# Tying GpSimd casts to VectorE instructions in an attention and feed-forward kernel, with a new order of steps

## The chip, the cores and the metric

One core of one Trainium2 chip. The metric is the device time in microseconds (us) of one execution; three runs of the kernel before took 270.18, 269.0 and 268.93 us, median 269.0 us. One further execution was recorded by the profiler; all durations below are from that one.

The core has a matrix engine (PE), a vector engine (VectorE, DVE in the profile), a scalar engine (ScalarE, ACT), a general engine (GpSimd, POOL) and a queue engine (SyncE, SP) which here only issues DMAs. Each engine works through its own list of instructions strictly in order; semaphores join the lists.

## The reference

Attention over 4 batches x 8 heads, 768 positions, head size 64, with a block mask (blocks of 32: neighbours, first and last rows and columns, three sampled blocks per row), then a feed-forward layer on the 3072 tokens of width 512:

```python
scores = np.where(mask, scale * q @ k.T, -1e9)          # per batch and head
attn = exp(scores - max) / (sum + 1e-9)
x = (attn @ v)                                          # 3072 x 512, heads side by side
h = x @ w_in                                            # 512 -> 2048
g = h / (1 + exp(-beta * h))
out = g @ w_out                                         # 2048 -> 512
```

## The kernel before, in words

**Pairs and units.** The 32 heads are worked in 16 pairs (two heads side by side in the 128 partitions). The query rows of a batch are cut in two tiles of 256 and 512 rows; one pair's one tile is a *unit*, numbered 0 to 31 in the order of work. Feed-forward groups are numbered 100 to 106 (100 has 256 tokens, 101 to 105 have 512, 106 has 256).

**What one pair needs first** (`add_prep`, `add_half`, `add_load`, `add_cast`): k, q and v of the pair are loaded by DMA from the SP queue into float32 staging buffers `st_k` (4 of them), `st_q` (3), `st_v` (2). A *cast* (`add_cast`, its instruction on line 509 when GpSimd does it) makes float16 of each: `s16_k` and `s16_q` (the trace calls them s_k, s_q) or `va` (v). For pairs 0 to 3 PE transposes s_k and s_q and a copy puts them in `kX`, `qX` ("turn", "turn cp"); for the later pairs a transposing DMA on the SP queue does it (`turn` in `add_half`, line 524). A staging buffer can be loaded anew once its cast is done, so a cast also lets a later load go. The first later loads are held back by one-element GpSimd copies ("shut", line 489), which wait for the weights `w_out` to land.

**A unit** (`tile_steps`, `add_step`, `add_tail`): PE makes scores `sc` from kX and qX ("sc", 64 rows deep); ACT takes the exponential to `et` ("ex"); DVE multiplies `et` by the 0/1 mask ("mk": two float16 inputs, both in SBUF); PE multiplies by `va` ("av"); DVE takes the reciprocal of the sums and scales ("norm": its large input is in PSUM) to `xst`; a transpose brings that to `x`. The first four units add the mask on PE instead, with `shut_qk`.

**A feed-forward group** (`add_moe`, `add_mixed`): "hp" on PE (x by w_in, to PSUM), "th" on ACT (tanh), "gm" on DVE (`g`: one input t_sb in SBUF, the other in PSUM), then products with w_out. Groups 101 to 106 use a seven-product scheme for 2 x 2 blocks: DVE makes sums of halves ("sg": two SBUF inputs, one output of `s` or `g`) and, once, of the weights ("tw": two SBUF inputs, `w_mix` and `w_out_sb`); products ("pr") go to PSUM and are copied or added to `osb` ("cv", on ACT or DVE); the store goes by the SP queue (line 787).

**What sets the order.** No scheduler runs at build time. All steps are nodes with numbers; the table `STEPS` (from line 42) lists them in one sequence, and each engine gets its own steps in that sequence. A word of the table is the node's number, a letter for the engine (P PE, A ACT, D DVE, G GpSimd, S SP) and the buffer slots that it takes: `1041G3` is node 1041 on GpSimd in slot 3. `2V4`/`4W4` are filler matmuls on zeros (512 or 64 columns wide) near the start. Which engine does a step where two can (casts: D or G; PSUM copies: D or A) is thus also in the table. Helpers of class `Tap` record each PE, ACT and DVE instruction as it is emitted (line 185, which is why most instructions of the profile have that line); the GpSimd instructions are emitted directly.

**Nodes that the prediction names.** 54: cast of q of pair 3; 51 and 55: PE transposes of k and q of pair 3; 56: the copy of the latter to qX; 106, 107: last scores of unit 2 and their exponential; 113, 114: first scores of unit 3 and their exponential. 6: copy of a part of the mask on GpSimd (line 416); 209: a DVE copy to x; 236: the first "shut" copy; 237: the load of k of pair 4, 238 its cast on DVE. 620 and 623: casts of k and q of pair 8; 640, 641, 642: load, cast and transposing DMA of k of pair 9; 624: transposing DMA of q of pair 8; 669: the first scores that need it. 1041, 930, 927, 900: four casts which GpSimd does one after the other from 153.64 us on.

Of the kernel before, what the change touches and what calls it, by code (L numbers as in the profile page):

```python
# [42 lines left out]
11S0 15S0 19S 23S 27S1 0D 29S1 12D3 16G1 2V4 4W4 1P2 1W4 13P7 3D 2D 14A2 33S2 37S0 39S3 20G 43S1  # L43
1W4 17P6 18A 4W4 4P1 5D 1V4 4W4 80P3 81A2 7D 24D 2V4 1W4 21P0 22D 25P1 1V4 4W4 82P1 30D3 34D0 8D
26A 83Aa 28G1 47S1 1V4 2W4 84P0 85A0 31P7 32D0 38G2 9P5 35P4 44G0 36D 49S0 53S2 86P6 91P1 92A8
57S0 59S1 93P0 94Ad 87Db 10D 40D0 41P5 88D2 45P4 95P3 42D3 63S0 96A7 46D 104P1 102P0 89P5 103Ae
97P7 54G1 55P6 48D0 90A2 105A3 50D2 51P4 75G 76G 67S2 106P0 107A2 98De 99D0 100P7 52D1 56D 113P2
60D2 115P1 101D 117P3 61P0 62D 114A9 71S1 116A7 118Ab 108P1 184P1 185A2 68D1 64G0 65P0 187P2
109Dd 110D0 66D 193P3 69P1 190P1 77G 78G 79G 188Ad 58D3 119P4 186D 70D 196P0 189D 120Da 121D4
191A3 194A0 195D 199P3 122P2 111P5 112D 197A8 200Ab 210P2 123D 216P1 213P0 198D 201D 192D 211A7  # L50
212D 214Ae 215D 124P7 125A1 126D1 127P6 128A2 130P4 131A4 202P5 129D 133P1 217A6 132D 203D8
204D1 205P0 206Df 207D 136P6 134A4 135D 219P1 137A1 72D2 218D 138D 139P7 142P0 145P5 151P4 220Aa
140A5 143A3 141D 148P3 146A0 144D 152A5 149A6 147D 73P2 74D 153D 150D 221D 222P3 223A8 225P0
154P5 155A2 156D 224D 157P4 158A6 159D 226Ab 227D 169P2 160P7 170A1 161A5 162D 163P5 208P6 166P3
209D2 167A2 168D 247P0 164A3 165D 248A5 6G 236G2 237S 228P4 229D7 253P3 231P3 250P0 230D1 171D
256P2 254Ad 255D 232De 233D 251A8 249D 252D 172P2 257A4 258D 262P0 259P3 260Aa 240G0 178P3 173P
263A9 281P3 284P2 282A0 287P0 179P 174P 180P 261D 363D 364D 244G0 241S 296P3 238D1 367D 365D
283D 285Ae 290P2 288A2 264D 286D 293P0 239S3 297Ac 294A7 291A3 245S 273S3 175P 181P 268P1 265P7
234P6 176A1 235A 182A0 242D2 298D 289D 243S 276S0 279S1 295D 292D 299P2 368D 269Dc 266D3 267D2
270D 300D9 301D3 246G0 274G3 275S0 307S0 183S 310S2 302P0 404P2 407P3 303D7 304D 305P2 271P3  # L60
405A4 410P0 413P2 366D 306D 272D 318P3 315P2 408A5 406D 409D 369D 321P6 411A3 412D 277D2 414Ab
419P2 416P0 316A2 278S 280D1 319A0 317D0 320D 324P7 308G3 309S2 322A5 417A8 323D 418D 415D 327P2
333P0 330P6 313S0 429S2 432S0 336P1 420Ac 437P2 325A4 326D 328A1 329D 440P1 421D 334A5 331A2
332D 339P7 337A1 311G1 312S 422P6 335D 338D 371D0 423D1 424D2 438A1 441A2 442D 340A3 341D 342P4
446P1 443P0 345P5 348P6 343A0 444Ad 351P7 449P0 314G3 430G1 344D 354P4 346A1 347D 439D 425P5
447Ae 452P1 349A5 352A6 450A6 462P0 448D 433G2 350D 357P6 353D 360P7 355A2 453Ab 465P1 463A0
468P0 358A5 451D 426Dg 427D 445D 356D 454D 464D 455P5 458P4 361A2 359D 466A7 469Ac 362D 474P1
471P3 472A8 456D7 457D1 459Db 460D 374D 377P5 477P0 475A9 431S1 435S0 434S 487P3 478Ad 370D 473D
470D 467D 476D 479D 380P4 381P 490P1 488Aa 489D 372D 375D 493P0 491A3 378P 480P6 494Ae 379A0
481D2 382D 482D4 496P1 497A1 499P0 483P7 388P 502P1 500Ab 596P0 484Dh 485D 593P3 503A5 385P  # L70
594Ad 597A8 386P 599P1 600A0 606P3 619S3 622S2 428S0 607A9 623G1 620D0 389P 387A 436G2 492D 383D
504D 498D 495D 501D 595D 598D 376D 373D 505P1 506D6 609P1 612P3 508P0 610A7 391P 613A4 509D0
507D2 510D 627P1 625S1 640S1 461S 643S0 486S 644G2 641G1 646S0 177S 390D1 628A6 633P0 634Ab
630P3 631Ae 392P 601D 602P3 626G0 384D 614D 393D 603D8 604D0 394P 648P3 661S0 664S1 665D0 649A5
651P1 652A1 629D 653D 654P0 655A0 395P 621S3 511S 515P6 516A0 512P7 513A1 642S2 624S 669P0 396D
672P1 673Aa 397P 670A3 518P4 519A5 632D 611D 514D1 605S1 667S1 645S 682S3 685S2 662G0 663S1 666S
683G2 686G1 684S0 524P3 525A2 521P1 522A6 527P0 656D 608D 517D 520D 528A1 526D 523D 529D 530P4
531A6 690P3 691A8 671D 532D 635D 675P1 398P 615P0 676Ac 399D 692D 402S 616D0 617D2 618S 687S
401S 533P4 534A1 535D 693P3 694Ad 695D 696P1 697A7 636P1 668G3 688S1 536P0 537A1 637Da 638D0
538D 677D 539P7 540A3 706P1 703P2 704A2 542P1 543A2 707A4 545P0 546A4 548P5 551P4 554P2 552A5  # L80
549A0 557P3 541D 544D 674D 650D 560D0 647G1 555A3 547D 716P0 709P3 553D 657P4 689G2 558A4 710A9
550D 678P5 717A0 556D 559D 722P1 658Dg 659D2 719P3 566P4 567P 810P0 723A1 816P1 720A6 813P3
811Aa 711D 563D 679Dd 680D3 569P5 698D 699P0 570P 561D 564D 705D 721D 700D9 701D1 817A5 819P1
814A8 825P0 822P3 820A3 400S 403S 568D0 574P 708D 712P3 573D 571D 577P 823Ae 835P3 660S 681S
# [133 lines left out]
def kernel(  # L218
# [11 lines left out]
    nc = tc.nc  # L230
# [770 lines left out]
```

## Time and profile before

| what | us |
|---|---|
| median of three runs | 269.0 |
| the profiled execution | 269.45 |
| its span, first to last instruction | 267.6 |
| PE busy | 255.8 |
| DVE busy | 234.1 |
| ACT busy | 208.0 |
| POOL busy (58 instructions) | 41.4 |

The span and the execution's time differ by 1.85 us, which lie around the span. The granted PE clock is 1.00 throughout. "Busy" of PE counts modelled ends of pipelined matmuls, so it says where PE stands idle, and not how well it is filled. In a row of the time-ordered view stand start, duration, engine, line, operation, output<-input with sizes and types, the count, and in square brackets the idle time ahead of it with what ended it.

### The profile page before, as it was taken

How to read it: one execution, taken by the hardware profiler on the slowest of the kernel's cores; microseconds unless marked ns; L12 is line 12 of the kernel's file. 1: busy time of each engine (PE TensorE's matmuls, PEld its weight loads, DVE VectorE, ACT ScalarE, POOL GpSimd, SP SyncE). 2: the span in 40 equal slices, each digit the busy share in tenths (PEclk: the TensorE clock that was granted, in tenths of full speed). 3: DMA queues.
4: the chain of work that ended last, by engine and by line, in shares of the span. 5: the costliest groups of instructions: out<-in, count | busy, mean ns of one | idle time of the engine just before them, and what ended most of it. 6: DMA issues, size and time to landing. Idle time of an engine off the chain costs nothing.

```text
span 267.6 us, 6834 instructions
## 1 busy us (share of the span) xinstructions
PE 255.8 (96%) x2796; PEld 167.6 (63%) x2796; DVE 234.1 (87%) x483; ACT 208.0 (78%) x277; POOL 41.4 (15%) x58
## 2 busy tenths in 40 slices
PE   8987999999998999999999979999999999999994
PEld 4664873634465765556775536746676875578883
DVE  5548999999999989999999999789989996999762
ACT  2789999799997989898889867987587895643330
POOL 4334001203233020500006060200010000000000
PEclk9999999999999999999999999999999999999999
DMA  6999996999892899954499816800261100202042
GB/s 186 294 204 207 211 207 155 212 244 235 168 276 68 237 123 192 173 186 118 101 168 230 217 20 153 143 11 0 58 200 31 23 4 0 71 20 100 0 159 78
DMA packets 72979, 36.70 MB, mean 137 GB/s; under 512 B 29796, under 2 KB 68980, under 8 KB 72948
## 3 DMA queue, kind: packets, MB, share of 16 engines
q1 hardware_dynamic: 69744, 32.06, 52.4%
q0 software_dynamic: 3136, 4.19, 9.2%
q8 instruction: 22, 0.36, 0.6%
q14 instruction: 9, 0.07, 0.1%
q10 hardware_dynamic: 68, 0.01, 0.0%
HBM read 27.27 MB, written 6.29 MB: 125 GB/s over the span
## 4 chain that ended last, share of the span: by engine, by line
PE 71%; DVE 17%; ACT 6%; DMA 2%; issue 1%; POOL 0%; DVEq 0%; ACTq 0%; POOLq 0%
PE sc L185 71%; DVE et L185 6%; DVE g L185 4%; ACT et L185 3%; ACT t_sb L185 3%; DMA st_q<-in_q_dram 2%; DVE s L185 2%; DVE xst L185 2%; DVE w_mix L185 1%; DVE w_out_sb L185 1%; DVE recip L185 1%; DVE x L185 0%; DVE s_q L185 0%; DVE osb L185 0%; ACT osb L185 0%
## 5 line engine op out<-in xcount | busy, mean ns | idle before, releaser
L185 ACT ACTIVATE et<-sc 128x1024 f16<-128x1024 f32 x144 | 139.1, 1039 | 17.5 <-PE sc L185 16.3
L185 PE MATMUL sc<-x,w_in_sb 128*128 128x512 f16 (+1 forms) x448 | 90.1, 349 | 1.9 <-DVE g L185 1.7
L185 DVE TENSOR_TENSOR et<-et,mask 128x960 f16<-128x960 f16 (+1 forms) x132 | 85.7, 679 | 4.7 <-ACT et L185 4.7
L185 ACT ACTIVATE t_sb<-sc,beta_c_sb 128x512 f16<-128x512 f32 (+1 forms) x112 | 65.5, 644 | 25.6 <-PE sc L185 22.1
L185 DVE SCALAR_TENSOR_TENSOR g<-t_sb,sc 128x512 f16<-128x512 f16 (+1 forms) x112 | 64.0, 604 | 8.3 <-ACT t_sb L185 8.0
L185 PEld LDWEIGHTS <-w_in_sb 128*128 128x128 f16 x448 | 41.8, 98 | 40.4 <-issue 7.5
L185 PEld LDWEIGHTS <-g 128*128 128x128 f16 x505 | 47.1, 99 | 19.8 <-issue 9.2
L185 PE MATMUL sc<-w_out_sb,g 128*128 128x256 f16 (+1 forms) x384 | 50.9, 282 | 0.2 <-DVE xst L185 0.2
L185 PE MATMUL sc<-qX,kX 64*128 64x256 f16 (+1 forms) x384 | 45.6, 326 | 1.6 <-ACT et L185 0.8
L185 PEld LDWEIGHTS <-et 128*128 128x128 f16 x1152 | 40.9, 98 | 6.8 <-issue 3.2
L185 PE MATMUL sc<-va,et 128*128 128x65 f16 x1152 | 43.3, 193 | 1.3 <-ACT et L185 0.7
L185 PEld LDWEIGHTS <-kX 64*128 64x128 f16 x384 | 16.3, 94 | 18.5 <-issue 14.1
L509 POOL CAST va<-st_v 128x768 f16<-128x768 f32 x13 | 12.5, 963 | 88.9 <-PE sc L185 58.0
L185 PE MATMUL sc<-w_mix,s 128*128 128x256 f16 x176 | 22.1, 273 | 0.7 <-ACT osb L185 0.5
L185 DVE TENSOR_TENSOR xst<-sc,recip 128x256 f16<-128x256 f32 x48 | 19.7, 421 | 1.2
L185 PEld LDWEIGHTS <-s 128*128 128x128 f16 x176 | 16.2, 98 | 5.4 <-issue 3.7
L509 POOL CAST s_q<-st_q 128x768 f16<-128x768 f32 (+2 forms) x13 | 11.7, 901 | 21.1 <-DMA st_q<-in_q_dram 17.2
L185 ACT COPY osb<-sc 128x512 f32<-128x512 f32 (+2 forms) x14 | 7.5, 539 | 8.5 <-PE sc L185 8.5
L509 POOL CAST s_k<-st_k 128x768 f16<-128x768 f32 (+1 forms) x11 | 9.9, 904 | 24.1 <-DMA st_k<-in_k_dram 24.1
L185 DVE TENSOR_TENSOR osb<-osb,sc 128x512 f32<-128x512 f32 (+1 forms) x18 | 11.4, 635 | 2.2 <-ACT osb L185 1.4
L185 PE MATMUL sc<-w_mix,g 128*128 128x256 f16 x88 | 11.1, 273 | 0.0
L185 DVE RECIPROCAL recip<-sc 128x4 f32<-128x4 f32 x48 | 8.1, 173 | 2.9 <-PE sc L185 2.7
(66 smaller groups left out, 106.2 us busy)
## 6 DMA issues: line engine op xcount, KB each, us to landing
st_v<-in_v_dram SPq DMA_DIRECT2D x16, 384.0 KB, 4.3
out_dram<-osb SPq DMA_DIRECT2D x23, 256.0 KB, 2.5
st_k<-in_k_dram SPq DMA_DIRECT2D x15, 384.0 KB, 4.8
st_q<-in_q_dram SPq DMA_DIRECT2D x12, 384.0 KB, 4.8
w_in_sb<-in_moe_w_in_dram POOLq DMA_DIRECT2D x2, 1024.0 KB, 10.9
w_out_sb<-in_moe_w_out_dram POOLq DMA_DIRECT2D x2, 1024.0 KB, 19.2
st_q<-in_q_dram SPq DMA_DIRECT2D x12, 128.0 KB, 5.7
st_k<-in_k_dram SPq DMA_DIRECT2D x3, 128.0 KB, 2.5
```

Source lines behind the costliest of these rows:

```text
L185: r = f(*a, **kw)
L509: e(out=at(dst)[:, :, :, 0:D] if nm == "v" else by_chunk(dst, lo, hi), in_=src)
```

## The change

Three things. GpSimd instructions of the casts and of the mask copies are recorded too (`pool`). While the steps are emitted, the last DVE instruction so far is kept in `after`; a GpSimd cast or mask copy then gets a dependency on it, so that it can't start before that DVE instruction is done. And the whole table STEPS is another one: nearly the same sequence, in which steps of all engines stand a few places earlier or later, other buffer slots are taken, and some steps change engine. The core of the diff:

```diff
+    pool = Tap(nc.gpsimd, log)
...
-            e = dve if eng == "DVE" else nc.gpsimd
+            e = dve if eng == "DVE" else pool
...
-            e = dve.tensor_copy if eng == "DVE" else nc.gpsimd.tensor_copy
+            e = dve.tensor_copy if eng == "DVE" else pool.tensor_copy
...
+    after, told = None, mybir.DependencyInfo(mybir.DependencyClass.Sync,
+                                             mybir.DependencyReason.DATA)
     with tc.manual_schedule():
         emit_first()
         for n in seq:
...
+            if n.on == "DVE":
+                after = log[-1]
+            elif n.on == "POOL" and n.port and log and after is not None:
+                tc.add_manual_dep(log[0], after.name, told, reason="beside PSUM readers")
```

Of the table, the lines around the steps that the prediction names (before, then after):

```diff
-97P7 54G1 55P6 48D0 90A2 105A3 50D2 51P4 75G 76G 67S2 106P0 107A2 98De 99D0 100P7 52D1 56D 113P2
+40D2 57S1 91P3 93P2 92A0 94A2 86P1 87Da 59S0 41P0 45P7 95P1 42D1 46A 63S1 96Ad 102P2 106P3 103Ac
+88D1 104P0 50D3 89P3 97P2 67S2 76G 60G0 51P5 55P4 90D0 98D5 99D4 105Ab 52D3 77G 78G 79G 56A
+107A1 113P1 114Aa 71S0 115P0 117P2 116A6 118A0 61P6 100P7 108P2 58D3 64D1 65P3 62D 184P0 101D
...
-209D2 167A2 168D 247P0 164A3 165D 248A5 6G 236G2 237S 228P4 229D7 253P3 231P3 250P0 230D1 171D
+166P7 221D 223A1 224D 155A0 156D 158A2 159D 226Ab 227D 167A4 169P6 208P5 160P4 161A5 162D 209D2
+247P0 163P3 228P2 6G 236G3 237S 248A9 168D 253P2 250P0 231P7 170A2 164A1 229D8 230D2 254A7 171D
...
-270D 300D9 301D3 246G0 274G3 275S0 307S0 183S 310S2 302P0 404P2 407P3 303D7 304D 305P2 271P3
+279S0 307S2 274G1 275S1 295D 246G1 308G3 277G2 175P 176A0 180P 181P 182A1 268P2 365D 269Dc 368D
...
-775A0 770D 873D 889P2 758D 886P4 761D 864G0 865S 589S 773D 1015P0 1040S1 1041G3 930G0 592S 834S0
-859S 1043S0 591S 916P3 1016A2 927G0 928S0 1042S2 764D 917Ac 776D 783P5 1021P0 1022Ae 887Dd 888D1
+755D 756P3 746D 857Dg 899S1 862S3 926S1 927G3 591S 865S 929S0 932S0 834S1 592S 589S 928S0 895S1
+858D 759P0 767D 768P1 914Aa 915D 757A3 758D 897G2 771P2 762P3 774P7 930G0 885D 898S 911A2 769A4
+760A2 772A0 761D 770D 773D 763A3 764D 775A4 886P0 887Dh 776D 889P6 900G3 888D3 890Dd 891D 777D0
```

Steps that change engine: fifteen casts and copies of the first 40 us change between ACT and DVE or between DVE and GpSimd. Later, seven casts of whole k, q or v (128 x 768) go from GpSimd to DVE (436, 623, 644, 689, 861, 1041, 1047) and three from DVE to GpSimd (277, 280, 665); eight copies of a PSUM result (128 x 512) to osb go from DVE to ACT and three from ACT to DVE; one smaller one and two of three copies to x go from ACT to DVE, the third from DVE to ACT. The load order on the SP queue is the same for the first 18 loads. The fillers go from 7 wide and 21 narrow ones to 5 wide and 26 narrow ones. The number of matmuls that do work, of exponentials, multiplications and DMAs is the same.

More of the change, by code (lines that the diff above doesn't have):

```diff
@@ L120 @@
[L120 to L125 removed]
+11S3 12D3 0D 15S2 16D1 19S 23S 24G 20G 27S0 29S2 33S0 37S1 5W5 13P4 4V5 1W5 1P7 3D 14D0 2W5 9P0
@@ new lines @@
+1116P1 1119P0 1117D3 1118D4 1120D0 1121D 1234P3 1235Ad 1237P2 1238A5 1003P 1122P0 994D 1005P
+1244P3 1207D 1123D 1247P0 1250P2 1245Aa 1006P 1248A0 1239D 1210D 1213D 1214P6 1004D 1215Da
+1216D3 1220D 1007D 1236D 1223D 1124P1 1125A6 1127P7 1145P0 1128A0 1146A3 1251A3 1157P3 1008P
+1139P6 1166P4 1126D1 1226D 1233D 1129D 1158A2 1147D 1227P0 1136P5 1130P1 1228D2 1249D 1229D1
+1159D 1167A1 1217S2 1142P7 1140A6 1141D 1131A3 1137A4 1132D 1240P0 1241Db 1009P 1010A 1138D
+1143A4 1133P3 1169P2 1170A5 1134A2 1154P1 1252D 1242D4 1246D 1243S 1230S 1253P0 1168D 1160P4
```

144 lines of the change are left out of this document (66 added, 78 removed).

## The prediction

> **What bounds the kernel now.** I read the page's busy shares, its chain that ended last, that chain in order of time, and wherever it leaves PE, the time-ordered rows of DVE and POOL.
>
> ```profile
> PE 71%; DVE 17%; ACT 6%; DMA 2%; issue 1%; POOL 0%; DVEq 0%; ACTq 0%; POOLq 0%
> ...
> 85.19 64.41 PE sc L185 x712
> ...
> 164.87 31.34 PE sc L185 x282
> ...
> 202.54 56.35 PE sc L185 x604
> ```
>
> From 85 us on, PE sets the end in long runs (start, length), and what lies between them is what can be won. The largest hole of PE there is 1.73 us ahead of 159.61; DVE, POOL and PE around it (start, duration, engine):
>
> ```profile
> 152.68 1.27 DVE L185 SCALAR_TENSOR_TENSOR g<-t_sb,sc 128x512 f16<-128x512 f16 x2
> 153.98 1.03 DVE L185 TENSOR_TENSOR s<-g 128x1024 f16<-128x1024 f16 x1
> 155.05 1.20 DVE L185 TENSOR_TENSOR s<-s,g 128x1024 f16<-128x1024 f16 x1
> 156.16 1.27 DVE L185 TENSOR_TENSOR et<-et,mask 128x960 f16<-128x960 f16 x1
> 157.36 0.17 DVE L185 RECIPROCAL recip<-sc 128x4 f32<-128x4 f32 x1
> 157.45 1.18 DVE L185 TENSOR_TENSOR et<-et,mask 128x960 f16<-128x960 f16 x1
> ...
> 160.08 0.64 DVE L185 TENSOR_TENSOR et<-et,mask 128x960 f16<-128x960 f16 x1
> ...
> 153.64 0.83 POOL L509 CAST s_k<-st_k 128x768 f16<-128x768 f32 x1 [8.92 <-DMA st_k<-in_k_dram]
> 154.41 1.29 POOL L509 CAST s_q<-st_q 128x768 f16<-128x768 f32 x1
> 155.64 1.29 POOL L509 CAST s_k<-st_k 128x768 f16<-128x768 f32 x1
> 156.87 1.25 POOL L509 CAST va<-st_v 128x768 f16<-128x768 f32 x1
> ...
> 159.61 1.67 PE L185 MATMUL sc<-x,w_in_sb 128*128 128x512 f16 x7 [1.73 <-DVE g L185]
> ```
>
> A multiplication of `et` takes 0.64 alone (160.08) but 1.27 and 1.18 beside casts; a cast takes 0.83 alone and 1.25 to 1.29 beside DVE's work on two SBUF inputs. They take turns: the cast of 153.64 ends at 154.47, and the sum that DVE began at 153.98 ends 0.54 after that, so it did its work only then; the next cast, begun at 154.41, ends 0.69 after that sum. DVE instructions with their large input in PSUM pay nothing: the two g of 152.68 take 1.27 together with a cast beside the second, and the recip 0.17. So a chain of GpSimd casts stops DVE again and again, here where PE waits for g.
>
> **The change part by part.**
>
> *The chain of four casts, 153.6 to 158.1.* First the row of an undisturbed sum, and those of the next places:
>
> ```profile
> 77.32 0.68 DVE L185 TENSOR_TENSOR s<-g 128x1024 f16<-128x1024 f16 x1
> 77.92 1.31 DVE L185 TENSOR_TENSOR w_out_sb<-w_out_sb 128x1024 f16<-128x1024 f16 x1
> 79.15 4.12 DVE L185 TENSOR_TENSOR et<-et,mask 128x960 f16<-128x960 f16 x6
> ...
> 82.76 0.78 PE L185 MATMUL sc<-va,et 128*128 128x65 f16 x19 [0.36 <-DVE et L185]
> ...
> 45.34 0.55 DVE L185 CAST s_k<-st_k 128x768 f16<-128x768 f32 x1
> ...
> 60.00:85.00 25.00, 24.20 (x257) 13.35 (x256) 24.59 (x45) 24.14 (x33) 7.67 (x8) 1.00 0.89 203
> ...
> 150.00:165.00 15.00, 13.27 (x151) 7.65 (x148) 14.57 (x27) 11.00 (x16) 4.48 (x4) 1.00 0.45 127
> ```
>
> (In the last two: stretch, length, then busy time of PE, PEld, DVE, ACT, POOL.) DVE loses 1.03 - 0.68 + 1.20 - 0.68 = 0.87 on the sums and 1.27 - 0.64 + 1.18 - 0.64 = 1.17 on the multiplications, 2.04 in all. In the new table 1041 is DVE's and later; 927 is gated by a recip, with its xst and a g next; 897 and 930 by a g, with one multiplication and then three g next; 900 by a g, with recips and xst next. Behind such a gate the multiplication has begun when the cast comes, so the cast waits and DVE doesn't. I expect 0 to 0.3 of blocking here, so 1.73 to 2.04 won, as PE stands idle for 1.73: I take 1.8. Next in line would be ACT, with 11.00 busy of these 15 us, so it isn't late.
>
> *38 to 85 us.* DVE is full and ACT nearly (24.59 and 24.14 of 25). Two casts block DVE at 77.92 (1.31 for 0.68) and in the six multiplications after it: 4.12, where six undisturbed ones make 3.5 (6 x 0.64, less an overlap of 0.07 at five places: the row of 160.08 against starts 0.57 apart, an estimate). That is 0.63 + 0.62 = 1.25 lost, and PE waits for `et`. In the new order no cast stands there. But at 51 us four casts (274, 246, 308, 277) now stand behind multiplications, with a subtraction of weights, a recip and another subtraction next: two blockings of 0.63, the same 1.25, lost. These cancel. What stays is that 277 and 280 leave DVE ahead of 85 us (0.55 each, 0.48 less overlap: 0.95), while 436 and 623 come to it behind that. ACT allows less, idle 0.86 in 25 us. Bounds 0 and 1.2; I take 0.5, nearest to ACT's row.
>
> By the Trainium skill (SBUF — State Buffer, Who interferes with whom) DVE and GpSimd share one port pair, and whichever starts first has it for its whole instruction while the other is fully blocked. By that rule each blocking at 51 us would cost DVE a whole cast, an estimate of 2 x 0.83 = 1.66 instead of 1.25, and the sum below would be -2.1 instead of -2.5. The trace's blockings cost 0.34 to 0.63, as a blocked instruction was issued while its predecessor, or the cast, was already under way; the sum keeps to the rows.
>
> *The start.*
>
> ```profile
> 15.65 1.08 ACT L185 ACTIVATE et<-sc 128x1024 f16<-128x1024 f32 x1
> 18.02 2.85 ACT L185 ACTIVATE et<-sc 128x1024 f16<-128x1024 f32 x3 [1.28 <-PE sc L185]
> ...
> 16.75 0.28 PE L185 MATMUL sc<-identity,s_q 128*128 128x128 f16 x2 [1.15 <-POOL s_q L509]
> ```
>
> ACT, without a gap from 18 to 29 us, stands idle 1.28 ahead of that because scores 106 are queued on PE behind transpose 55, which waits for cast 54 and its load. The new table puts 106 ahead of 51 and 55, but on ACT copy 56 now stands ahead of exponential 107. 55 runs at 16.75 to 17.03, copy 56 about 0.4 after that, 107 then 0.9 (three follow each other in 2.85): exponential 114 can start near 18.35, where it was second after 18.02, at 18.9. Won 0.55, bounds 0 and 1.0 (other gates may move the load); I take 0.5. The fillers and small copies lie under waits for the first loads, like this one; uncovered, five more narrow and two fewer wide fillers would change less than 0.3 either way.
>
> *The mask copy that now waits.*
>
> ```profile
> 22.32 0.75 POOL L416 COPY mask<-mask_kb 128x384 f16<-128x384 f16 x1
> 37.52 0.51 POOL L489 CAST st_k<-w_out_sb 1x1 f32<-1x1 f16 x1 [14.44 <-DMA w_out_sb<-in_moe_w_out_dram]
> ...
> 38.05 0.37 SPq L480 DMA_DIRECT2D st_k<-in_k_dram  x1
> ...
> 38.48 0.33 DVE x L185
> ...
> 44.76 0.57 issue
> ...
> st_k<-in_k_dram SPq DMA_DIRECT2D x15, 384.0 KB, 4.8
> ```
>
> Copy 6 ran at 22.32. Now it waits for 209 (38.48, done 38.81), then takes 0.75, and behind it on POOL is 236, behind that load 237, and on DVE cast 238 (45.34), ahead of which the chain already holds 0.57 without work. So the load goes at 39.6 instead of 38.05. With the median 4.8 to landing it is there at 44.4: no loss. With the 7.3 that it took (45.34 - 38.05, beside the weights) it is there at 46.9: 1.5 lost on the bounding engine. The weights' DMAs stand earlier on POOL now, so less runs beside it: I take 0.3.
>
> *The waits themselves.* A hop from DVE to POOL isn't in the trace; the nearest rows are the chain's pieces without work, 0.57 at the most, and it is POOL that pays, with 7.67 busy of 25 us in the row above. Queued behind a waiting cast are the casts after it, their transposing DMAs on SP, and the next load of the same staging buffer. This costs nothing as long as all come ahead of the scores that need them: rival 3.
>
> *Engine moves.* From 40 to 160 us five casts come to DVE and three leave, and three output copies leave: 2 x 0.55 - 3 x 0.68 (an output copy is as long as a sum on the nearest row), -0.9 of DVE, under PE's runs. ACT takes the three; it has slack after 85. Later moves lie under PE's runs of 31.34 and 56.35. Bounds -0.9 and +0.5; I take 0.
>
> *Sum.* -1.8 - 0.5 - 0.5 + 0.3 = -2.5. The profiled execution took 269.45, its span of 267.6 and 1.85 around it; so 266.95. It stood 0.45 over the median of the three runs, so **266.5** against 269.0.
>
> **The rivals.**
>
> 1. *The forecast: the chain at 153 goes, the rest is small.* 266.5, own range 264.7 to 268.0 (gains of 2.04 + 1.2 + 1.0 without loss give 264.8; 1.73 won and 0.7 lost elsewhere give 268.0). For it: blocking and idle time are of one size, at one place.
>
> 2. *The blocking moves, or the wait isn't what decides.* The cast of 153.64 started when its load landed (8.92 of waiting), not when POOL was free: if loads land late, casts start beside whatever runs, gate or none. And in the new order some nine casts still have two-SBUF-input work next, at 0.3 to 0.6 each. If half of the 2.04 comes back where PE is about to wait, and the start and the mask copy cancel, 0.5 to 1.0 is won: 268.0 to 268.5, with a full return 269.0; I take 268.5.
>
> 3. *Slower: prefetch too late through the SP queue.* Place: 86 to 100 us. DVE's cast 620 frees the buffer that load 640 takes; cast 641 waits for the load and a gate, 642 waits for 641 on SP, and 624, the q that scores 669 need, is queued on SP behind 642.
>
> ```profile
> 85.94 0.55 DVE L185 CAST s_k<-st_k 128x768 f16<-128x768 f32 x1
> ...
> 90.29 1.98 SPq L524 DMA_TRANSPOSE kX<-s_k  x1
> ...
> 100.24 0.61 PE L185 MATMUL sc<-qX,kX 64*128 64x256 f16 x8
> ...
> DMA to landing us min/median/max: 2.8/3.8/6.0
> ```
>
> (85.94 is 620, 100.24 is 669, the last row is for the qX transposes.) With the medians, 86.5 + 4.8 + cast 1.3 + issue of 642 2.0 + 3.8 = 98.4, against 100.24 less the gains of 1.0: 0.8 in time, and it decides from there on. With 7.3 and 6.0 it is 103.1, and PE waits 3.9. DVE then gains a lead, so the hole at 159 goes as well: -1.0 + 0.3 + 3.9 - 1.8 = +1.4, or 270.4; with 238 late by its full 1.5, 271.6. Middle: 271.0. In the old order 641 was a GpSimd cast without gate. Against it: both DMAs must be near their worst.
>
> **How the numbers follow.** Forecast 0.57, rival 2 0.24, rival 3 0.19. A measurement can tell about 0.5% from no change, here 1.35 us: below 267.65 is faster, above 270.35 slower. Below lie nine tenths of the forecast and a fifth of rival 2: 0.56. Slower: rival 3, 0.19. The rest, 0.25, is the same. For 8 in 10 the range leaves out a twentieth below the forecast's lower end, 264.7, and half of rival 3 above: 270.8.
>
> **What would show it.** Right: PE's wait ahead of 159.6 is gone; multiplications and sums of 1.0 to 1.3 are fewer than half as many; casts start right behind DVE instructions; ACT's hole ahead of 18 is half as long or less. Wrong: PE idle for kX or qX between 95 and 105; DVE idle by more than 0.6 ahead of its first s_k cast behind 40; new blockings next to PE's waits for g.

## The result and the profile after

The kernel after takes **266.34 us** (median of four, 266.1 to 266.63) against 269.11 us (268.93 to 270.18) in runs side by side: a ratio of 0.989, with a 95% interval from 0.986 to 0.9918. That is 2.8 us faster; the prediction was 266.5. The profiled execution took 266.1 with a span of 264.3, so 1.8 lie around the span, as before. The granted PE clock is 1.00 again. One execution among the experiments (scores 669 one step later) took 292.56 us at a mean granted clock of 0.85 and is left out of that kernel's figures.

From the page of the kernel after, busy times, the chain that ended last, and the group of multiplications (count, then busy us and mean ns, then idle time ahead); recorded instructions now have line 184, GpSimd's casts too:

```profile
PE 254.3 (96%) x2799; PEld 166.6 (63%) x2799; DVE 228.7 (87%) x483; ACT 208.6 (79%) x279; POOL 35.4 (13%) x56
...
PE 69%; DMA 9%; DVE 9%; ACT 6%; SPq 2%; issue 2%; POOL 0%; DVEq 0%; POOLq 0%
...
L184 DVE TENSOR_TENSOR et<-et,mask 128x960 f16<-128x960 f16 (+1 forms) x132 | 82.1, 653 | 0.8 <-ACT et L184 0.6
```

The same group in the kernel before:

```profile
L185 DVE TENSOR_TENSOR et<-et,mask 128x960 f16<-128x960 f16 (+1 forms) x132 | 85.7, 679 | 4.7 <-ACT et L185 4.7
```

The same 132 multiplications take 3.6 us less, as few of them are still blocked (of the multiplications, sums and subtractions, ten took 1.0 us or more before and one does now); POOL's busy time is 6.0 less (41.4 before), in part because it has fewer casts. In the chain, DMA's share rose from 2 to 9%, so more of what sets the end is now a transfer.

Where the time went is seen from three stretches (start and end, length, busy time of PE, PEld, DVE, ACT and POOL, then PE's granted clock). The kernel before, whose stretch of 150 to 165 us the prediction shows:

```profile
62.00:92.00 30.00, 29.01 (x341) 17.59 (x340) 29.68 (x56) 28.39 (x37) 7.77 (x8) 1.00 0.80 190
92.00:113.00 21.00, 21.00 (x236) 13.16 (x233) 19.33 (x38) 18.98 (x24) 6.23 (x6) 1.00 1.04 176
```

The kernel after:

```profile
62.00:92.00 30.00, 29.88 (x367) 18.82 (x367) 29.60 (x61) 29.23 (x37) 5.47 (x6) 1.00 0.72 180
92.00:113.00 21.00, 20.42 (x207) 11.64 (x205) 18.95 (x36) 18.82 (x25) 4.47 (x5) 1.00 1.06 194
...
150.00:165.00 15.00, 15.00 (x172) 9.00 (x169) 13.58 (x28) 12.60 (x18) 3.62 (x4) 1.00 0.93 185
```

PE's idle time goes from 0.99 to 0.12 us in the first stretch and from 1.73 to nothing in the last, and from nothing to 0.58 in the middle one: a gain, a loss and a gain.

The place of the old hole, in order of time, in the kernel after:

```profile
153.05 0.83 POOL L184 CAST s_k<-st_k 128x768 f16<-128x768 f32 x1 [12.08 <-DVE recip L184]
155.35 1.96 POOL L184 CAST s_q<-st_q 128x768 f16<-128x768 f32 x2 [1.47 <-DVE g L184]
160.34 0.83 POOL L184 CAST va<-st_v 128x768 f16<-128x768 f32 x1 [3.02 <-PE sc L184]
...
155.21 0.65 DVE L184 TENSOR_TENSOR et<-et,mask 128x960 f16<-128x960 f16 x1
156.97 2.48 DVE L184 SCALAR_TENSOR_TENSOR g<-t_sb,sc 128x512 f16<-128x512 f16 x4 [1.11 <-ACT t_sb L184]
...
154.76 3.40 PE L184 MATMUL sc<-x,w_in_sb 128*128 128x512 f16 x15
158.00 1.69 PE L184 MATMUL sc<-va,et 128*128 128x65 f16 x48
```

PE runs from the hp steps into the av steps with no idle time in brackets. The casts start behind a recip and a g, as the waits want it, the multiplication beside them takes its undisturbed 0.65 while one of the two casts of 155.35 waits for it (1.96 for both, where two alone take about 1.6), and DVE is ahead by so much that it waits 1.11 for ACT. The new holes of PE:

```profile
99.63 0.61 PE L184 MATMUL sc<-qX,kX 64*128 64x256 f16 x8 [0.39 <-DMA qX<-s_q]
...
111.14 0.61 PE L184 MATMUL sc<-qX,kX 64*128 64x256 f16 x8 [0.19 <-DVE g L184]
...
255.63 1.91 PE L184 MATMUL sc<-w_mix,s 128*128 128x256 f16 x16 [0.52 <-DVE osb L184]
```

The first is at the scores 669, for the transposing DMA 624.

### The profile page after: what moved, and what is told of

Read it like the earlier page. It is cut to its first block, busy times and chain, and to the rows that moved or that the text cites. A ratio compares the mean times of both kernels' runs of the same rounds, so it can differ in the third digit from the quotient of the medians.

```text
span 264.3 us, 6872 instructions
## 1 busy us (share of the span) xinstructions
PE 254.3 (96%) x2799; PEld 166.6 (63%) x2799; DVE 228.7 (87%) x483; ACT 208.6 (79%) x279; POOL 35.4 (13%) x56
## 4 chain that ended last, share of the span: by engine, by line
PE 69%; DMA 9%; DVE 9%; ACT 6%; SPq 2%; issue 2%; POOL 0%; DVEq 0%; POOLq 0%
PE sc L184 69%; ACT et L184 4%; DMA st_q<-in_q_dram 4%; DMA w_in_sb<-in_moe_w_in_dram 4%; DVE et L184 3%; DMA qX<-s_q 2%; DVE xst L184 2%; ACT t_sb L184 2%; DVE g L184 1%; DVE w_mix L184 1%; SPq L480 1%; SPq L483 1%; DVE recip L184 1%; DVE osb L184 1%; SPq L524 0%
## 5 line engine op out<-in xcount | busy, mean ns | idle before, releaser
L184 DVE TENSOR_TENSOR et<-et,mask 128x960 f16<-128x960 f16 (+1 forms) x132 | 82.1, 653 | 0.8 <-ACT et L184 0.6
L184 PEld LDWEIGHTS <-w_in_sb 128*128 128x128 f16 x448 | 41.4, 98 | 39.0 <-issue 5.7
L184 POOL CAST s_k<-st_k 128x768 f16<-128x768 f32 (+1 forms) x10 | 8.1, 814 | 77.6 <-DVE recip L184 30.5
L184 ACT COPY osb<-sc 128x512 f32<-128x512 f32 (+2 forms) x18 | 9.8, 571 | 9.8 <-PE sc L184 9.8
L184 POOL CAST s_q<-st_q 128x768 f16<-128x768 f32 (+2 forms) x13 | 10.2, 790 | 39.8 <-DVE g L184 28.6
L184 POOL CAST va<-st_v 128x768 f16<-128x768 f32 x11 | 10.2, 935 | 18.4 <-DVE g L184 7.6
```

What stands on the lines that cost most here:

```text
L184: r = f(*a, **kw)
```

## The experiments

**PE's lag.** The kernels have different orders, so the same place of the work comes at different times. For a step of PE I take its start less the sum of the matmul time that stands ahead of it in PE's own order (each step at the cost that the kernel's node list gives it). This *lag* stays constant while PE runs one kind of step without a gap, and grows by each wait, each small gap and each stretch at a lower granted clock. The table gives the lag at step 124 (near 27 us), and then by how much it has grown at later steps (about 72, 89, 113, 153, 160, 165 and 260 us). The last column is the median time of the runs of that kernel, for the two kernels of the case that of the runs side by side. The lags of a row are from one profiled execution, the median is from four to twelve.

| kernel | at 27 | 72 | 89 | 113 | 153 | 160 | 165 | 260 | median us |
|---|---|---|---|---|---|---|---|---|---|
| before | 10.59 | 3.64 | 6.57 | 7.99 | 10.31 | 12.19 | 12.72 | 16.11 | 269.11 |
| after | 9.93 | 3.75 | 5.20 | 7.71 | 9.79 | 9.80 | 10.15 | 13.34 | 266.34 |
| new order, no waits | 10.21 | 4.21 | 5.58 | 8.47 | 10.62 | 10.63 | 10.98 | 14.16 | 267.23 |
| old order, all waits | 12.52 | 4.61 | 6.11 | 9.57 | 12.15 | 12.15 | 16.23 | 31.62 | 286.34 |
| before, waits on four casts | 9.70 | 3.64 | 6.58 | 8.00 | 10.46 | 10.46 | 10.85 | 14.27 | 266.81 |
| before, g 767 first | 10.01 | 3.64 | 6.51 | 8.24 | 10.53 | 10.53 | 11.98 | 15.32 | 268.10 |
| before, four casts swapped | 10.36 | 3.64 | 5.32 | 7.96 | 10.25 | 12.41 | 12.94 | 16.36 | 268.95 |
| before, scores 106 first | 10.18 | 3.65 | 6.96 | 8.47 | 10.76 | 12.54 | 13.07 | 16.41 | 269.22 |
| after, q 624 first | 10.76 | 5.10 | 6.55 | 8.96 | 11.04 | 11.05 | 11.40 | 14.59 | 266.27 |
| after, scores 669 later | 9.96 | 4.95 | 6.40 | 8.98 | 11.05 | 11.06 | 11.41 | 14.60 | 266.76 |
| after, no waits at 62 to 72 | 10.09 | 4.32 | 5.70 | 7.86 | 9.93 | 9.94 | 10.29 | 13.48 | 267.34 |
| after, no waits at 105 to 117 | 10.16 | 3.94 | 5.39 | 8.23 | 10.32 | 10.33 | 10.68 | 13.87 | 266.43 |
| after, those nine waits alone | 10.76 | 3.89 | 5.35 | 7.60 | 9.67 | 9.68 | 10.03 | 13.20 | 266.51 |
| after, tail swapped | 10.71 | 5.25 | 6.70 | 9.65 | 11.72 | 11.74 | 12.09 | 14.59 | 266.42 |

By the first two rows the kernel after grows 2.77 less (16.11 - 13.34): 0.28 of it up to 113 us, 0.24 up to 153, 1.87 at the old hole, and 0.38 behind it. That the medians also differ by 2.77 is a coincidence: the spans of the two profiled executions differ by 3.3, as step 124 stands 0.94 earlier (26.43 for 27.37) and what follows step 1324, the last one in the table, takes 0.43 longer (6.07 for 5.64).

How much the growth differs where nothing was edited is seen from rows with the same order. Up to 113 us the kernel before and the two that differ from it only behind 150 us have 7.99, 8.00 and 8.24; from 89 to 113 the kernel after has 2.51 and the one with the tail swapped, which is the same up to there, 2.95. So the 0.28 is not clear of this scatter. From 113 to 153 all rows with the new order have 2.07 to 2.15 and those with the old order, but for the one with all waits, 2.29 to 2.46, and the 1.87 is larger than any scatter. The rest of this section asks what made these pieces. The median of the kernel before, run beside the experiments, was 269.07 (18 runs), 269.2 (23) and 269.08 (11) in the three groups.

**My theory** after the result: the chain of casts blocked VectorE ahead of g 767, and that this is gone gives two thirds of the gain. **Rivals:** that VectorE's new order, and not the casts, took the hole away; and that the waits did it or had no part in it.

### The new table without the waits

```diff
-            if n.on == "DVE":
-                after = log[-1]
-            elif n.on == "POOL" and n.port and log and after is not None:
-                tc.add_manual_dep(log[0], after.name, told, reason="beside PSUM readers")
```

> The changed kernel without the dependencies: the new table alone. Theory (the waits keep the casts beside PSUM readers): casts start when their loads land, DVE's blocking goes back from about 2 to 5 or 6 us, and a good part of it reaches PE: 267.3 to 268.3, with PE again idle by 0.8 or more near 157. Rival (order and engine moves alone made DVE early enough): 266.0 to 266.7, whatever the blocking. A third way: faster than the changed kernel, 265.5 to 266, since casts come earlier and scores 669 no longer wait for their q.

Measured: 267.23 (266.61 to 267.95), ratio 0.9931 with an interval from 0.9905 to 0.9956. The table alone brings 1.8 of the 2.8 us, and the hole ahead of 159.61 is gone without any wait (growth 10.62, then 10.63), which the theory didn't expect; nor is it the rival's time. GpSimd at that place, and then VectorE and PE near 70 us, where this kernel loses:

```profile
150.31 0.83 POOL L184 CAST s_k<-st_k 128x768 f16<-128x768 f32 x1 [8.57 <-DMA st_k<-in_k_dram]
151.07 0.84 POOL L184 CAST s_q<-st_q 128x768 f16<-128x768 f32 x1
153.22 0.83 POOL L184 CAST s_q<-st_q 128x768 f16<-128x768 f32 x1 [1.32 <-DMA st_q<-in_q_dram]
...
67.72 1.85 DVE L184 TENSOR_TENSOR et<-et,mask 128x960 f16<-128x960 f16 x2
...
71.42 0.61 PE L184 MATMUL sc<-qX,kX 64*128 64x512 f16 x4 [0.37 <-DVE g L184]
```

In the new order the casts start as soon as their loads land, and that happens to be beside three g and two small instructions, which read PSUM: each cast takes its undisturbed 0.83. At 67.72 two multiplications take 1.85 instead of 1.28, and PE then waits for g.

### The old table with the waits

```diff
 STEPS: the table of the kernel before
+            if n.on == "DVE":
+                after = log[-1]
+            elif n.on == "POOL" and n.port and log and after is not None:
+                tc.add_manual_dep(log[0], after.name, told, reason="beside PSUM readers")
```

> The kernel before with the dependencies: the old table, whose places for some casts were never meant as start times. Theory (a wait is worth only what the place that it names is worth): q cast 864 now starts behind g 761, done near 161.8, its transposing DMA lands near 166.5, and scores 1015 that stood at 163.0 are 3 us late; q cast 1044 behind g 978 (198.8), landing near 204, for scores 1098 of 198.6, 5 us late; less the hole at 159.6: 272 to 278. Rival (the wait is the gain): 266.5 to 267.5.

Measured: 286.34 (286.08 to 286.91), ratio 1.0639 (1.0604 to 1.0675); PE's clock was granted at 0.97 on average. Slower, as expected, and by more than expected. Two of PE's largest holes, PE's clock behind the first (the 0.50 in the third row), and cast 1041:

```profile
167.47 0.61 PE L185 MATMUL sc<-qX,kX 64*128 64x512 f16 x4 [2.56 <-DMA qX<-s_q]
...
213.77 1.46 PE L185 MATMUL sc<-qX,kX 64*128 64x512 f16 x6 [5.13 <-DMA qX<-s_q]
...
168.50:171.50 3.00, 3.00 (x15) 1.31 (x14) 2.54 (x4) 2.53 (x4) 1.08 (x2) 0.50 1.05 268
...
170.42 1.05 POOL L185 CAST s_k<-st_k 128x768 f16<-128x768 f32 x1 [5.86 <-DMA st_k<-in_k_dram]
```

Scores wait for a transposing DMA, a third time for 2.73 ahead of 179.02, so 10.4 in all. Behind each of the three waits the granted clock is 0.50 (168.5 to 171.5, 179 to 181.5 and 214 to 219 us), and the lag grows there by another 5 (1.4, 1.3 and 2.3). Together that is about the 15.5 by which this kernel's lag grows more than the kernel before's (31.62 for 16.11); what brought the clock down was not tested. In the old table the casts stand far down the sequence, so a wait for the last VectorE instruction ahead of a cast is a wait for a late one. A cast lets the next load of its staging buffer go, so a late cast makes a later one late: 1041 starts at 170.42 instead of 153.64, and it is its load that it waits for. The hole at 157 us is gone here too (growth 12.15 and 12.15). It is rival 3's mechanism, at another place.

### Waits on the four casts alone

```diff
 STEPS: the table of the kernel before
+            if n.no == 770:
+                after = log[-1]
+            elif n.no in (1041, 930, 927, 900):
+                tc.add_manual_dep(log[0], after.name, told, reason="beside PSUM readers")
```

> The kernel before, with a wait for these four GpSimd casts alone (1041, 930, 927, 900): each waits until g 770 is done, near 160 us, so that none of them runs beside the sums and multiplications of 153 to 158 us; VectorE's order is that of before. Theory that the blocking makes the hole: the two sums take 0.68, the two multiplications 0.65, g 767 ends 2.0 earlier, the hole ahead of 159.61 is 0 to 0.2, the lag at 160 us is 1.5 to 1.7 less; if kX and qX still come in time for the scores at 174 to 178 us, 267.3 to 267.7; each scores step that comes late gives back up to the 2.6 to 2.7 that the late scores cost where every cast waited. Rival (the order on VectorE alone makes the hole): over 1.0 of the hole stays and the time is 268.5 or more.

Measured: 266.81 (266.26 to 267.28), ratio 0.9907 (0.9881 to 0.9934). VectorE's order is that of before, to the last instruction. VectorE, GpSimd and PE at the place:

```profile
153.25 0.69 DVE L185 TENSOR_TENSOR s<-g 128x1024 f16<-128x1024 f16 x1
...
154.58 0.65 DVE L185 TENSOR_TENSOR et<-et,mask 128x960 f16<-128x960 f16 x1
...
156.12 1.27 DVE L185 SCALAR_TENSOR_TENSOR g<-t_sb,sc 128x512 f16<-128x512 f16 x2
...
157.46 1.19 POOL L185 CAST s_k<-st_k 128x768 f16<-128x768 f32 x1 [13.62 <-DVE g L185]
...
154.82 4.05 PE L185 MATMUL sc<-x,w_in_sb 128*128 128x512 f16 x18
```

The sums take 0.69 instead of 1.03 and 1.20, the multiplication 0.65 instead of 1.27, g 767 and 770 start at 156.12 instead of 158.89, and PE goes through its 18 hp matmuls without a hole. The growth from 153 to 160 us falls from 1.88 to 0, and 1.84 is still there at the end: nothing gives it back. So the blocking made the hole, and taking it away in the old order is enough. By the lag, four waits win about as much here (1.84) as the whole new table does without any (1.95). The median is 2.4 less than that of the kernel before, below the 267.3 to 267.7 of the theory; what the difference from 1.84 comes from stays open.

### g 767 first, casts as they were

```diff
-766A3 777D0 778D 909D 857D8 906D 858D 767D 759P1 769A6 757A1 760A2 771P0 772A4 762P5 763A3 774P3
-775A0 770D 873D 889P2 758D 886P4 761D 864G0 865S 589S 773D 1015P0 1040S1 1041G3 930G0 592S 834S0
+766A3 777D0 778D 857D8 858D 767D 759P1 769A6 757A1 760A2 771P0 772A4 762P5 763A3 774P3
+775A0 770D 873D 909D 906D 889P2 758D 886P4 761D 864G0 865S 589S 773D 1015P0 1040S1 1041G3 930G0 592S 834S0
```

> The kernel before, with the two multiplications 909 and 906 moved on VectorE behind the g steps 767 and 770 and multiplication 873; the four GpSimd casts of 153.64 to 158.1 stay where they are, without a wait. Theory (the hole of 1.73 us ahead of 159.61 is set by what stands on VectorE ahead of g 767; the new table takes it away by putting 767 ahead of the sums and multiplications): the blocked sums still cost 0.87, but g 767 ends near 157.4 instead of 159.5, ahead of PE's need at 157.88, so the hole is 0 to 0.2, the lag of PE from 160 us on is 1.5 to 1.7 less, and the time is 267.3 to 267.7. Rival (the chain of casts is what decides, wherever g stands): VectorE stays 2 us late, PE waits 1.0 to 1.7 at the next product or exponential instead, and the time is 268.4 to 269.1.

Measured: 268.1 (267.59 to 268.74), ratio 0.9954 (0.9935 to 0.9973): between the two. VectorE, then PE:

```profile
153.63 1.09 DVE L185 TENSOR_TENSOR s<-g 128x1024 f16<-128x1024 f16 x1
...
156.43 1.27 DVE L185 SCALAR_TENSOR_TENSOR g<-t_sb,sc 128x512 f16<-128x512 f16 x2
...
161.25 0.61 PE L185 MATMUL sc<-qX,kX 64*128 64x512 f16 x4 [0.27 <-DVE g L185]
163.54 0.39 PE L185 MATMUL sc<-qX,kX 64*128 64x512 f16 x2 [0.34 <-DVE xst L185]
```

The hole ahead of step 762 is gone (10.53 and 10.53), as the two g start at 156.43 instead of 158.89; but the sums are still blocked, VectorE is still late, and PE waits a little later for another g and an xst. From 160 to 165 us the lag grows by 1.45, where it grew by 0.53 before. About half of 1.88 comes back, and 0.8 stays. Here an order that puts the urgent step first moves the cost of a blocking and doesn't remove it.

### Four casts changed between the engines

```diff
-... 411A3 412D 277D2 414Ab
-419P2 416P0 316A2 278S 280D1 319A0 ...
+... 411A3 412D 277G2 414Ab
+419P2 416P0 316A2 278S 280G1 319A0 ...
-... 607A9 623G1 620D0 389P 387A 436G2 492D 383D
+... 607A9 436D2 623D1 620D0 389P 387A 492D 383D
```

> The kernel before, without waits, with four casts changed between the engines as in the kernel after: 277 and 280 go from VectorE to GpSimd at their places (near 58 us), 436 and 623 from GpSimd (77.5 to 79.9) to VectorE, just ahead of cast 620 (near 85.5). Theory (the 1.0 to 1.4 us that the kernel after wins between 62 and 92 us come from these casts: 0.95 less on VectorE ahead of 70, no blocking of 1.25 at 77.9, 0.96 more behind 85): PE's lag is 0.5 to 0.95 less at 72 us, 1.2 to 2.2 less at 84 us, 0.8 to 1.3 less at 92 us, and what lasts to the end is 0.6 to 1.3: 267.8 to 268.5. Rival (the gain needs the waits and the new order of the other steps; 277 and 280 on GpSimd block VectorE as much as they free): less than 0.5 at 84 us and 268.9 to 269.3.

Measured: 268.95 (268.39 to 269.62), ratio 0.9989 (0.9973 to 1.0005): no change. VectorE, then PE:

```profile
77.69 0.69 DVE L185 TENSOR_TENSOR w_out_sb<-w_out_sb 128x1024 f16<-128x1024 f16 x1
...
89.89 0.81 PE L185 MATMUL sc<-va,et 128*128 128x65 f16 x20 [0.33 <-DVE et L185]
...
159.60 1.89 PE L185 MATMUL sc<-x,w_in_sb 128*128 128x512 f16 x8 [2.00 <-DVE g L185]
```

The theory is right up to 89 us, and the rival at the end. The blocking of 1.31 at 77.9 is gone, and the growth at 89 us is 1.25 less (5.32 for 6.57), what the theory gave. But the two casts now on VectorE stand ahead of the multiplications of 89 us, PE waits for those, and at 113 us all of it is back (7.96 for 7.99).

### Scores 106 ahead of transpose 55

```diff
-97P7 54G1 55P6 48D0 90A2 105A3 50D2 51P4 75G 76G 67S2 106P0 107A2 98De 99D0 100P7 52D1 56D 113P2
+97P7 54G1 106P0 55P6 48D0 90A2 105A3 50D2 51P4 75G 76G 67S2 107A2 98De 99D0 100P7 52D1 56D 113P2
```

> The kernel before with scores 106 moved ahead of transposes 55 and 51 on PE. Theory (ACT's hole of 1.28 ahead of 18.02 is scores queued behind a transpose that waits for a load, and ACT carries it to the end): ACT's hole shrinks by 0.8 or more, 268.2 to 268.7. Rival (DVE, full from 38 to 55, or the hole at 159.6 takes it back): 269.0 to 269.2.

Measured: 269.22 (268.36 to 269.71), ratio 1.0001 (0.9983 to 1.0018): no change. The row of ACT:

```profile
18.52 10.19 ACT L185 ACTIVATE et<-sc 128x1024 f16<-128x1024 f32 x11 [0.50 <-PE sc L185]
```

ACT's hole of 1.28 is down to 0.50, and PE's lag at 27 us is 0.41 less; by 89 us the growth is 0.39 more (6.96 for 6.57), in the stretch where VectorE is busy 29.68 of 30 us. So the rival's time is right. That VectorE took the gain back is not shown: the lag at 27 us differs from run to run without any edit ahead of it (9.70, 10.01, 10.36 and 10.59 in four profiled kernels with the old order there, 9.93 to 10.76 in six with the new order and all its early waits), and the two that started with 9.70 and 10.01 grew no more than the kernel before up to 89 us (6.58 and 6.51).

### The two places behind 95 us

First the transposing DMA 624 ahead of the DMA for x, in the kernel after:

```diff
-395P 654P3 648P2 661S3 486S 511S 642S1 624S 631Ab ...
+395P 654P3 648P2 661S3 486S 624S 511S 642S1 631Ab ...
```

> The changed kernel with one step moved on SP: the transposing DMA 624 of a q ahead of 511 instead of behind 511 and 642. Theory (scores 669 wait for 624, which queues on SP behind two DMAs that start late): 624 goes near 91 instead of 95.2, PE's wait ahead of 99.6 is gone, 0.3 to 0.6 less: 265.7 to 266.1. Rival (what PE wins there it loses at the next place, scores 706, or DVE is the bound at 100 to 111): 266.3, within 0.15.

Then the scores that wait for it, one step later, with two small moves on ACT and VectorE:

```diff
-652Ae 608D 653D 513A4 516A1 514D0 517D 650D 669P2 672P1 673A0 518P6 519A0 520D 524P7 525A6 521P2
+652Ae 608D 653D 513A4 516A1 514D0 517D 650D 518P6 669P2 672P1 519A0 673A0 520D 524P7 525A6 521P2
-636P3 637Df 638D0 616D4 617D1 400S 684S2 639S 618S 687S 535D 560D0 539P1 ...
+636P3 637Df 638D0 535D 616D4 617D1 400S 684S2 639S 618S 687S 560D0 539P1 ...
```

> The kernel after, with three moves behind 98 us: on PE the hp step 518 ahead of the scores 669, which wait for the transposing DMA of q; on ACT its tanh 519 ahead of the exponential 673; on VectorE g 535 ahead of the scaling 616 and 617. Theory (the waits of 0.39 ahead of 99.63 and 0.19 ahead of 111.14 are paid on the path, the place of the late transposing DMA): both go, and the time is 265.7 to 266.0. Rival (ACT, which limits VectorE from 98 to 104 us, is late next and takes it back): PE waits 0.2 to 0.5 at another step before 115 us and the time is 266.2 to 266.5.

Measured: 266.27 (265.4 to 268.1), ratio 0.9905 (0.9872 to 0.9938), and 266.76 (266.57 to 267.36), ratio 0.9911 (0.9883 to 0.9939). Neither shows a gain, though seven runs that differ by 2.7 can't rule out 0.3 to 0.6: two of the first kernel's took 265.40 and 265.48, less than any run of the kernel after. In the first, 624 starts at 95.09 and not near 91, as an earlier transposing DMA of x holds SP's queue from 91.56 for 3.43, and PE waits for x and an xst instead of q (two rows); in the second it waits for an exponential and an xst (two rows):

```profile
99.27 0.38 PE L184 MATMUL sc<-x,w_in_sb 128*128 128x512 f16 x1 [0.24 <-DMA x<-xst]
99.80 0.40 PE L184 MATMUL sc<-qX,kX 64*128 64x256 f16 x4 [0.15 <-DVE xst L184]
```

```profile
103.02 2.75 PE L184 MATMUL sc<-x,w_in_sb 128*128 128x512 f16 x12 [0.18 <-ACT et L184]
...
112.44 0.61 PE L184 MATMUL sc<-qX,kX 64*128 64x256 f16 x8 [0.37 <-DVE xst L184]
```

From 89 to 113 us the lag of the second grows by 2.58, where the kernel after grew by 2.51. So far as these two executions show, the place where the kernel after gives back 1.1 of its early lead is no single late transfer: SP's queue, ACT and VectorE come late one behind the other. The second kernel's growth at 72 us (4.95) is no work of its edit: ahead of it, at 63.55, PE waited 1.28 for another transposing DMA of a q, where it waited 0.12 in the kernel after. Such a DMA can thus land late in one execution and not in another.

### Which waits are worth the other 0.9 us

The kernel after, without the waits of the five casts of 62 to 72 us; without those of the four casts of 105 to 117; and with these nine waits alone:

```diff
-            elif n.on == "POOL" and n.port and log and after is not None:
+            elif ... and n.no not in (314, 311, 430, 433, 280):
+            elif ... and n.no not in (683, 686, 647, 668):
+            elif ... and n.no in (314, 311, 430, 433, 280, 683, 686, 647, 668):
```

> The kernel after, without the waits of the five casts that stand between 62 and 72 us (314, 311, 430, 433, 280); all other waits stay. Theory (the 0.9 that the waits are worth beside the new order, 267.23 against 266.34, sits at two places, here and at 105 to 117 us): the casts start near 66 again, multiplications beside them take 1.2 for 0.65, PE's lag is 0.4 to 0.7 more at 72 us than in the kernel after, and the time is 266.7 to 267.0. Rival (a lag made at 72 us is taken up by the next stretch, as with the kernels that moved one step near the start or near 98 us): the lag is the same again by 113 us and the time is 266.2 to 266.5.

> The kernel after, without the waits of the four casts that stand between 105 and 117 us (683, 686, 647, 668); all other waits stay. Theory: casts 647 and 668 start near 112 beside a sum and a multiplication, which take 1.1 to 1.25 for 0.68 and 0.62, PE's lag is 0.3 to 0.6 more at 118 us, nothing takes it back as PE runs without a gap from there to 255 us, and the time is 266.6 to 266.9. Rival (VectorE has slack here, PE doesn't wait for what is late): lag and time stay, 266.2 to 266.5.

> The kernel after with the waits of these nine casts alone (314, 311, 430, 433, 280 and 683, 686, 647, 668); all others, those of the casts at 150 to 160 us and near the start among them, go. Theory (these nine carry all that the waits win in the new order): 266.2 to 266.5, with no hole near 157 us, as the new order had none without any wait. Rival (the waits at 130 to 160 us or at the start are needed too, once the nine keep the order in time): 266.8 to 267.3.

Measured, in this order: 267.34 (266.47 to 268.2), ratio 0.9937 (0.992 to 0.9955); 266.43 (265.95 to 267.59), ratio 0.9902 (0.9882 to 0.9922); 266.51 (265.78 to 266.86), ratio 0.9898 (0.9882 to 0.9915). By the medians, and with intervals that lie apart from the last kernel's, the five waits of 62 to 72 us carry the 0.9 that the waits are worth beside the new order (267.23 without any, 266.34 with all), and the other waits, those at the old hole among them, carry nothing that can be measured. In the kernel without the four waits of 105 to 117 the casts block again (VectorE, then PE):

```profile
111.54 1.06 DVE L184 TENSOR_TENSOR s<-g 128x1024 f16<-128x1024 f16 x1
112.53 1.24 DVE L184 TENSOR_TENSOR et<-et,mask 128x896 f16<-128x896 f16 x1
...
111.89 0.61 PE L184 MATMUL sc<-qX,kX 64*128 64x256 f16 x8 [0.47 <-DMA qX<-s_q]
```

The sum and the multiplication take 1.06 and 1.24, but what PE waits for at that time is a DMA, and it doesn't wait for either of the two. The lag at 113 us is 0.52 more than in the kernel after, and stays so, which is the size that the theory gave. But the kernel with the tail swapped, which has all its waits, grew as much from 89 to 113 (2.95, here 2.84) and waited 0.64 for the same kind of DMA at the same scores 706. So this growth can't be put down to the casts.

One thing stays open here. In the one execution of the first kernel that was profiled, its fastest, the 0.6 that is lost at 72 us (4.32 for 3.75) is down to 0.15 by 113 us, as the rival has it, while the other five runs took 267.07 to 268.2, as the theory has it. No profile shows how these five went behind 72 us.

### The tail

```diff
-1203S 1204S 1305D 1308D 1290D 1314P7 1309D 1307D 1310D 1312P3 1311D 1313D1 1315D 1317D 1318P
+1203S 1204S 1305D 1308D 1290D 1312P3 1314P7 1309D 1307D 1310D 1313D1 1311D 1315D 1317D 1318P
```

> The kernel after, with the last group's product 1312 ahead of 1314 on PE and its copy 1313 ahead of sum 1311 on VectorE. In the kernel after PE waits 0.52 to 0.68 ahead of 255.63 for copy 1313 of the product that ran last. Theory (nothing stands behind this that could take it back, as all later steps hang on this product): the wait is 0 to 0.1, PE's lag at the end is 0.5 to 0.7 less, and the time is 265.6 to 265.9. Rival (sum 1315, which needs both products, comes later and the next product waits for it instead): 266.2 to 266.5.

Measured: 266.42 (265.54 to 268.1), ratio 0.9906 (0.9881 to 0.9932). PE at the place:

```profile
257.65 1.91 PE L184 MATMUL sc<-w_mix,s 128*128 128x256 f16 x16
```

The hole of 0.52 is gone, and from product 1199 to product 1324 PE's lag grows by 0.00, where it grew by 0.67 in the kernel after. But its median isn't lower than the kernel after's. The profiled execution, its slowest, lost 1.58 more than the kernel after between 27 and 33 us, where nothing was changed, as did the one with q 624 first. The cause there is PE's granted clock, 0.50 in this stretch (the first row; the kernel with q 624 first has 0.50 there too) and 1.00 in the kernel after (the second):

```profile
27.50:30.50 3.00, 3.00 (x28) 2.39 (x27) 1.90 (x4) 2.61 (x5) 0.00 (x0) 0.50 1.13 214
...
27.50:30.50 3.00, 3.00 (x62) 2.52 (x60) 2.74 (x8) 3.00 (x7) 0.00 (x0) 1.00 1.14 211
```

PE is busy for 3.00 in both, with 28 matmuls in the first and 62 in the second. What lowers the clock in some executions and not in others is open. So the mechanism is shown by the trace, the gain by no time: six runs that differ by 2.6 can't show 0.7.

## Why the prediction was right, point by point

**The chain of four casts, -1.8: right in cause and size.** The growth at that place is 1.88 before and 0.01 after, and waits on those four casts alone took 1.84 in the old order. VectorE came out of it early and waits 1.11 for ACT, the engine that the step named next in line. But the prediction let the waits do it, and in the new table they aren't needed: without any of them the casts stand beside g, recip and xst because of when their loads land and where they stand in the order. Here rival 2's doubt, that the gate isn't what decides, was right, though its outcome, a blocking that moves, came only in the kernel with g 767 first.

**38 to 85 us, -0.5: wrong in its parts.** The blocking at 77.9 went, as said. The 1.25 that were to come back at 51 us did not:

```profile
51.66 0.82 POOL L184 CAST s_k<-st_k 128x768 f16<-128x768 f32 x1 [9.27 <-DMA st_k<-in_k_dram]
...
57.80 0.83 POOL L184 CAST s_k<-st_k 128x768 f16<-128x768 f32 x1 [4.55 <-DMA st_k<-in_k_dram]
```

Two of the four casts waited for their loads until 57.8 and stood beside g there; the other two stood beside recips and xst; all took 0.83. I had taken the place in the order for the place in time. So the early lead was 1.37 at 89 us and not 0.5. Then the second failure: I let it stand, and 1.1 of it was given back by 113 us, at scores 669 and behind. What stayed is 0.28, no more than the scatter. By the medians the five waits of 62 to 72 us are worth 0.9, which the prediction had at nothing; by the lag of the one execution without them that was profiled, they are worth 0.14 at the end (13.48 for 13.34), and this stays open.

**The start, -0.5: not shown.** ACT's hole shrank (16.63 in the rows below), but the same move alone changed no time, and the lag at 27 us lies between 9.7 and 10.8 with either order.

**The mask copy, +0.3: it didn't happen.**

```profile
16.63 0.37 ACT L184 COPY qX<-sc 128x256 f16<-128x256 f16 x1 [0.69 <-DVE kX L184]
...
37.77 0.51 POOL L184 COPY mask<-mask_kb 128x384 f16<-128x384 f16 x1 [6.29 <-DVE x L184]
...
38.42 0.37 SPq L480 DMA_DIRECT2D st_k<-in_k_dram  x1
...
44.15 0.55 DVE L184 CAST s_k<-st_k 128x768 f16<-128x768 f32 x1
```

Copy 6 did wait for 209, but 209 was itself earlier (it ended at 37.70, not 38.81), the load went at 38.42 and not at 39.6, and cast 238 ran at 44.15, earlier than before.

**The waits themselves and the engine moves, 0.** No cost of the waits shows in the new order; in the old one they cost 17 us. The three output copies and the casts that changed engine show no price of their own: PE has no hole from 113 to 255 us.

**The sum.** -1.8 - 0.5 - 0.5 + 0.3 came to 266.5 where 266.34 was measured, with the largest term right and three small ones that were wrong or can't be seen in the scatter and cancelled; that it came within 0.2 is luck. The forecast's size is thus better founded for the hole (1.87 of 2.77) than for the rest.

**The rivals.** Rival 3's place was the right one to fear: PE waits 0.39 for the DMA of q at scores 669. It cost a part of the lead and no more, as that DMA wasn't near its worst; in the old order with waits the same mechanism costs 10.4 in three waits, and the lower clock behind them about 5 more.

**The signs named.** PE's wait ahead of 159.6 gone, VectorE's long multiplications and sums fewer than half (ten of 1.0 us or more before, one after), casts right behind VectorE instructions, ACT's hole halved: all seen. The wrong sign that did show, PE idle for qX between 95 and 105, marks the place where the lead was lost.

## What to carry to other kernels

Price a GpSimd cast by what stands beside it at the moment when its load lands, and not by its place in the order: beside instructions that read PSUM it was free here, beside those with two SBUF inputs it cost VectorE 0.3 to 0.6 us each time, and the end only where PE was about to wait for VectorE. Tie down just those casts, to an instruction with readers of PSUM behind it, if their transfers still come in time: four such waits took 1.84 out of the lag, with the first cast 3.8 us later, where the same wait on every cast in an order that wasn't made for it lost 17. A stretch in which three engines are full can give back what is won ahead of it, so add up the growth of the lag over the whole kernel before counting a hole as time. And look at the granted clock of each stretch before explaining a difference between two executions: here 0.50 over some 3 us made 1.5 us.

## What the runs showed of the hardware

By the Trainium skill (SBUF — State Buffer, Who interferes with whom) a VectorE instruction with at most one SBUF input doesn't contend with GpSimd outside the 2-port modes, and one with two contends with a GpSimd instruction that reads SBUF. The runs agree on who: beside casts a g, with one of its inputs in PSUM, took 0.68 as ever; in the prediction's rows a multiplication took up to 1.27 and a sum up to 1.20. The price, 0.34 to 0.63 where a cast takes 0.83, doesn't speak against a block that lasts until the other instruction ends: in the prediction's rows the sum begun at 153.98 ends 0.54 after the cast of 153.64, the next one 0.55 after the cast of 154.41, the multiplication behind it 0.50 after the cast of 155.64. Each of the three began 0.3 to 0.6 after its cast, so it paid the rest of the cast and not all of it. The full block that the prediction cites stands in that section of the Trainium skill for VectorE's 2-port modes; for two SBUF inputs it says only that they contend.

I had not expected what PE loses between kinds of matmuls. The kernel after, near 200 us, where PE waits for nothing:

```profile
199.20 1.92 PE L184 MATMUL sc<-w_out_sb,g 128*128 128x256 f16 x16
200.96 1.04 PE L184 MATMUL sc<-w_mix,s 128*128 128x256 f16 x8
201.93 0.83 PE L184 MATMUL sc<-qX,kX 64*128 64x512 f16 x10
```

Sixteen products take 1.76 to the next product's start, so 0.88 for eight; the eight ahead of scores take 0.97. Between 64-row scores and 128-row matmuls about 0.09 us goes each time, and PE's order has 132 such changes in either kernel, fillers left out: an estimate of some 12 us (132 x 0.09) of either, and most of the lag's growth where PE shows no idle time. No run here has fewer of them, so that they could be won is not shown.
